# Attention blocks of 32 queries by 64 keys, four above each other, with v on both halves of the rows; rows of a stage's first slot requested ahead of weights

## The chip, the cores and the metric

The kernel runs on one core of one Trainium2 chip. Its metric is the device time of one execution, in microseconds. Five engines work side by side, each through its own list of instructions in order: TensorE (PE, whose weight loads are shown apart as PEld), VectorE (DVE), ScalarE (ACT), GpSimd (POOL) and SyncE (SP). SP mostly issues DMA transfers. Tiles live in SBUF (128 rows, or partitions); PE writes its results into eight banks of PSUM, from which DVE and ACT read them.

## What is computed

The reference is an attention block whose output feeds a mixture of experts:

- q, k, v are (batch 8, heads 8, 576 tokens, 64). Heads 0 to 3 attend to the 32 latest tokens. Heads 4 to 7 attend within 128 tokens to every fourth one, so with the tokens of equal remainder by 4 (a "strip" of 144) put together they too attend to the 32 latest of a strip.
- `attn = softmax(q @ k.T / 8 + mask)`, `attn @ v`, and the heads side by side give x of 4608 tokens by 512.
- `logits = x @ w_gate`, the largest of 8 picks an expert e, with the softmax's value as gate; `y = gate * (relu(x @ w1[e]) @ w2[e])`, w1 512 by 1024, w2 1024 by 512, all in f32.

## The kernel before, in words

A unit of attention is one pair of heads of one batch; there are 32, four to a batch: two with the plain mask (`ty` 0) and two with the strips (`ty` 1). `attention()` runs them as a software pipeline: in step i it normalizes unit i-1 (`norm`), computes the scores of unit i (`front`), the weighted sum of v of unit i-3 (`summed`) and the gate logits of unit i-4 (`logit_part`), transposes the weights of unit i-2 (`weights`, LAG is 2), turns q and k of unit i+1 (`turn`), writes rows for unit i-3 (`row_part`) and takes the exponentials of unit i (`exponentials`).

In `front` (L368) a unit's two heads lie on the two halves of the rows. Each has nine blocks of 64 queries by 96 keys (64 and the 32 ahead of them). PE is used as four arrays of 64 by 64: head r picks the half of the rows, the block's number the half of the columns (`place`). A head has one PSUM bank. For batches below EARLY (4) the mask is added on PE ahead of the scores (L356), and the exponentials read PSUM; for later batches DVE adds it (L390) and the exponentials read SBUF. ACT takes one exponential for each of nine columns of blocks (L405), with the sum as a by-product; POOL multiplies by the reciprocals (L420). `weights` makes nine transposes of 128 by 96 in three banks (L430), DVE copies each bank (L432). `summed` multiplies each block with its 96 rows of v (L445), which `load_v` brought in (L274, L277 and L290, on SP); ACT copies the two banks into xT (L459, L466). The PSUM banks go round among all tiles named `bank`, seven of them.

When a batch has ended, `route(b)` finds each token's expert and place and scatters the rows, with gate and number, into `bucket` in DRAM (L234); it is a generator, and the driver runs one piece of it after each piece of attention. `tables(s)` then lists the slots of stage s: a slot is 128 rows of one expert. `moe()` runs the slots: transposes of the rows (`across`, L1136), ph (64 matmul records, L1204), py (16 records of 512 columns, L1236), and a scatter to the output on POOL (L1253). Two slots out of all mix experts (L1166).

The order around the change is set by two things. First, the pacer at the end: each `yield` of `attention()` states a cost, and between two of them expert work is run at a rate (`clock`), counted in those costs; a stage's slots are spread over a given sum of costs. Second, `wanted`, an ordered list of rows ("x") and weights ("w1", "w2", in halves of 1 MB) with the number of finished layer halves that each waits for; `fetch` issues from its head only, on SP (rows of the last slots on ACT). SP is one queue in order: q, k, v, rows and weights all stand in it as they were issued.

At the start POOL issues five DMAs: the masks, the constants `cst`, and the gate's weights `wg`.

Of the kernel before, what the change touches and what calls it, by code (L numbers as in the profile page):

```python
# [69 lines left out]
LAG = 2  # L70
# [9 lines left out]
def _constants():  # L80


    def band(j, ty):

        qi, ki = 64 * j + np.arange(64)[:, None], max(0, 64 * j - WIN) + np.arange(96)[None]
        seen = (qi - ki >= 0) & (qi - ki < WIN)
        if ty:
            seen &= qi // STRIP == ki // STRIP
        return np.where(seen, 0.0, BIG)

    def mask(ty):

        pairs = [(0, 1), (2, 3), (4, 5), (6, 7), (8, 8)]
        return np.concatenate([np.concatenate([band(j, ty) for j in two]) for two in pairs], 1)
# [4 lines left out]


    parts = {"add0": mask(0)[:, 0:384], "add1": mask(1)}
    for name, ty, js in (
        ("even0", 0, (0, 2, 4, 6, 8, 8)), ("even1", 1, (0, 2, 4, 6, 8)), ("odd1", 1, (1, 3, 5, 7, 8))
    ):
        parts[name] = np.tile(np.concatenate([band(j, ty) for j in js], 1), (2, 1))
    parts["turn"] = np.tile(np.eye(64), (2, 1))

    exact, mask_at = [], {}
    for names in (("turn", "even0"), ("even1", "odd1"), ("add0", "add1")):
        n = 0  # L110
        for name in names:
            mask_at[name] = len(exact), n
            n += parts[name].shape[1]
        some = np.concatenate([parts[name] for name in names], 1).astype(np.float32)
        exact.append(np.ascontiguousarray(some.astype(ml_dtypes.bfloat16)))
    mask_at["odd0"] = mask_at["even0"][0], mask_at["even0"][1] + 96
# [45 lines left out]
def kernel(  # L162
# [91 lines left out]

    t = {}
# [12 lines left out]
    def first_key(j):  # L268
        return max(0, 64 * j - WIN)

    def load_v(b, ty):
        if ty == 0:
            x = pool.tile([96, 4, 9, DH], F32, tag="v0", name=f"v0_{b}", bufs=1)
            nc.sync.dma_start(x[:, :, 0, :], v[b, 0:4, 0:96, :].rearrange("h p d -> p h d"))  # L274
            for h in range(4):
                a = v[b, h, 64 - WIN : 160 - WIN, :]
                nc.sync.dma_start(  # L277
                    x[:, h, 1:9, :],
                    bass.AP(a.tensor, a.offset, [[DH, 96], [64 * DH, 8], [1, DH]]),
                )  # L280
        else:
            x = pool.tile([96, 2, 9, 2 * DH], F32, tag="v1", name=f"v1_{b}", bufs=1)
            for j in range(9):
                lo, end = first_key(j), first_key(j) + 96
                while lo < end:
                    hi = min(end, (lo // STRIP + 1) * STRIP)
                    h, m, at0 = lo // (2 * STRIP), lo // STRIP % 2, lo % STRIP
                    a = v[b, 4 + h : 5 + h, DIL * at0 + 2 * m : DIL * at0 + 2 * m + 1, :]
                    p0 = lo - first_key(j)
                    nc.sync.dma_start(  # L290
                        x[p0 : p0 + hi - lo, :, j, :],
                        bass.AP(
                            a.tensor,
                            a.offset,
                            [[DIL * DH, hi - lo], [2 * S * DH, 2], [1, 2 * DH]],
                        ),
                    )
                    lo = hi
# [39 lines left out]
    def place(r, j):  # L338

        return (4, r) if j == 8 else (5 * r + j // 2, j % 2)  # L340
# [3 lines left out]
    for j in range(0, 8, 2):  # L344
        ORDER += [(0, j), (1, j + 1), (0, j + 1), (1, j)]
    ORDER += [(0, 8), (1, 8)]

    def front(qT, kT, ty, early):
# [3 lines left out]
        for r in range(2) if early else ():  # L352
            rows = slice(DH * r, DH * r + DH)
            for c in range(2):
                n = 480 if c == r else 384
                nc.tensor.matmul(  # L356
                    sc[r][64 * c : 64 * c + 64, 0:n],
                    lhsT=mask("turn", rows, 64),
                    rhs=mask(("even", "odd")[c] + str(ty), rows, n),
# [4 lines left out]
        ends = [[max(j for j in range(9) if place(r, j)[1] == c) for c in range(2)] for r in range(2)]  # L364
        for r, j in ORDER:
            i, c = place(r, j)
            rows = slice(DH * r, DH * r + DH)
            nc.tensor.matmul(  # L368
                sc[r][64 * c : 64 * c + 64, 96 * (i % 5) : 96 * (i % 5) + 96],
                lhsT=qT[rows, 64 * j : 64 * j + 64],  # L370
                rhs=kT[rows, first_key(j) : first_key(j) + 96],
                start=not early,
                stop=not early or j == ends[r][c],
            )
        e = pool.tile([128, 9, 96], F32, tag="e", name="e", bufs=LAG + 1)
# [3 lines left out]
        for r in range(2):  # L379
            for i, n, p0, p1 in ((5 * r, 4, 0, 128), (4, 1, 64 * r, 64 * r + 64)):  # L380
                places.append((i, n, p0, p1, sc[r][p0:p1, 96 * (i % 5) : 96 * (i % 5 + n)]))
        for i, n, p0, p1, s in places:
            if early:
                nc.vector.tensor_reduce(  # L384
                    out=lo[p0:p1, i : i + n], in_=s.rearrange("p (i k) -> p i k", k=96),
                    axis=AX, op=OP.min,
                )
            else:
                at0 = 96 * (1 if (i, ty) == (4, 0) else i % 5)
# [3 lines left out]
                    in1=mask(f"add{ty}", slice(p0, p1), 96 * n, at0),  # L393
# [7 lines left out]
    def exponentials(e, lo, places):  # L401
        den = pool.tile([128, 9], F32, tag="den", name="den", bufs=3)
        for i0, n, p0, p1, s in places:
            for i in range(i0, i0 + n):
                nc.scalar.activation(  # L405
                    out=e[p0:p1, i],
                    in_=s[:, 96 * (i - i0) : 96 * (i - i0) + 96],
# [7 lines left out]
    def norm(e, den):  # L415
# [4 lines left out]
        nc.gpsimd.tensor_tensor(  # L420
# [938 lines left out]
```

## Time and profile before

| | us |
|---|---|
| median of 3 runs (842.04 to 842.5) | 842.38 |
| the profiled execution | 802.63 |
| its span, first to last instruction | 800.9 |
| PE busy in the span | 748.6 |
| DVE, ACT, POOL busy | 284.6, 225.5, 146.4 |
| granted TensorE clock, mean | 0.975 |
| attention alone, to unit 16's scores | 128.2 |
| attention and slots, from there to unit 31's scores | 300.2 |
| the rest | 372.5 |

The profile is of one execution, shorter than the timed runs; sums are made against its own time. A line of the groups names the source line, engine, operation, the tiles written and read, shapes, count, the busy time and the mean of one. On PE an f32 matmul stands as two records, each with a weight load; records overlap, so the distance from start to start tells more than the mean of one. In the table of windows each engine has its busy time and its instructions, then come the granted clock, DMA's busy share of 16 engines and GB/s.

### The profile page before, as it was taken

What the parts mean: (1) busy time and instruction counts of PE and PEld (TensorE: products, weight loads), DVE (VectorE), ACT (ScalarE), POOL (GpSimd) and SP (SyncE); (2) the same over time, 40 slices, a digit from 0 to 9 for tenths busy, and PEclk for the clock granted to TensorE, in tenths of its full rate; (3) what the DMA queues carried; (4) which work ended last, traced back from release to release, by engine and by line L of the source; (5) the groups of instructions that cost most, each with busy time, mean ns of one, the idle gap of its engine ahead of it and who ended that gap; (6) DMA issues with size and microseconds to landing.
All of it is one profiled execution on the core that took longest, in us unless ns stands there. A gap on an engine that the chain in (4) does not pass through costs nothing.

```text
span 800.9 us, 18005 instructions
## 1 busy us (share of the span) xinstructions
PE 748.6 (93%) x6838; PEld 559.4 (70%) x6838; DVE 284.6 (36%) x954; ACT 225.5 (28%) x853; POOL 146.4 (18%) x142
## 2 busy tenths in 40 slices
PE   4898898799997799999999999999999999999993
PEld 3787687488775577777777777768677374677681
DVE  1677878267334432354334411361101101101010
ACT  1896694253332132333333111000000011010000
POOL 1324433123211211113111300150000000000000
PEclk9999999899999799999999999999999999999997
DMA  9878689889999996799416937999992492993996
GB/s 200 178 157 196 156 233 370 190 242 281 281 305 279 359 265 193 253 311 313 147 58 199 279 122 228 309 355 383 328 319 82 150 330 97 320 307 122 332 309 219
DMA packets 164955, 195.39 MB, mean 244 GB/s; under 512 B 72720, under 2 KB 86688, under 8 KB 164866
## 3 DMA queue, kind: packets, MB, share of 16 engines
q1 hardware_dynamic: 153156, 169.00, 69.7%
q0 software_dynamic: 6928, 20.53, 7.2%
q10 hardware_dynamic: 4782, 4.67, 2.1%
q8 instruction: 57, 0.93, 0.5%
q14 instruction: 32, 0.26, 0.1%
HBM read 216.14 MB, written 21.54 MB: 297 GB/s over the span
## 4 chain that ended last, share of the span: by engine, by line
PE 79%; DMA 8%; ACT 5%; DVE 3%; issue 2%; another core or an unknown queue 1%; SPq 1%; POOL 0%; POOLq 0%; DVEq 0%; ACTq 0%
PE ph L1204 30%; PE py L1236 29%; PE xo L445 3%; ACT e L405 3%; PE scores L368 3%; PE weights L430 2%; DMA k<-in_k_dram 2%; DMA v<-in_v_dram 2%; PE xt L1136 2%; PE xrow L543 2%; DMA x<-bucket 2%; PE ph L1166 2%; PE py L1166 2%; PE turned L319 1%; DMA w<-in_moe_w_dram 1%
## 5 line engine op out<-in xcount | busy, mean ns | idle before, releaser
L1204 PEld LDWEIGHTS ph<-xt,w 128*128 128x128 f32 x2240 | 262.4, 193 | 19.5 <-issue 18.4
L1204 PE MATMUL ph<-xt,w 128*128 128x128 f32 x2240 | 271.7, 277 | 0.1
L1236 PE MATMUL py<-w,h 128*128 128x512 f32 x560 | 255.0, 598 | 0.0
L1236 PEld LDWEIGHTS py<-w,h 128*128 128x128 f32 x560 | 101.0, 191 | 101.4 <-issue 100.2
L1253 POOL DMA_INDIRECT out_dram<-y,to x35 | 34.6, 988 | 355.0 <-ACT y L1247 327.3
L1138 DVE COPY xt<-xt 128x512 f32<-128x512 f32 x38 | 26.1, 688 | 184.5 <-PE xt L1136 184.4
L1247 ACT ACTIVATE y<-py,x 128x512 f32<-128x512 f32 x35 | 24.0, 687 | 239.9 <-PE py L1236 177.6
L420 POOL TENSOR_TENSOR e<-e,rec 128x864 f32<-128x864 f32 x32 | 52.2, 1632 | 156.0 <-DVE rec L419 81.2
L432 DVE COPY eT<-weights 96x384 f32<-96x384 f32 x96 | 47.5, 545 | 39.8 <-PE weights L430 35.4
L405 ACT ACTIVATE e<-e,lo 128x96 f32<-128x96 f32 x144 | 51.8, 362 | 16.4 <-DVE lo L397 14.8
L234 POOL DMA_INDIRECT bucket<-rows,idx x48 | 44.5, 927 | 61.2 <-DVE idx L646 45.6
L405 ACT ACTIVATE e<-scores,lo 128x96 f32<-128x96 f32 (+1 forms) x160 | 52.5, 344 | 5.2 <-DVE lo L384 4.5
L445 PE MATMUL xo<-eT,v 96*64 96x64 f32 (+1 forms) x1216 | 45.2, 229 | 4.1 <-DMA v<-in_v_dram 4.1
L1224 DVE TENSOR_SCALAR h<-ph 128x512 f32<-128x512 f32 x35 | 24.1, 689 | 67.9 <-PE ph L1204 67.5
L445 PEld LDWEIGHTS xo<-eT,v 96*64 96x64 f32 x1216 | 40.5, 143 | 10.4 <-issue 6.6
L1215 ACT ACTIVATE h<-ph 128x512 f32<-128x512 f32 x35 | 20.8, 595 | 89.4 <-PE ph L1204 85.5
L312 ACT COPY kT<-turned 128x288 f32<-128x288 f32 x64 | 23.0, 414 | 80.2 <-PE turned L319 62.6
L430 PE MATMUL weights<-ident,e 128*96 128x128 f32 x288 | 39.2, 283 | 0.3 <-POOL e L420 0.3
L368 PE MATMUL scores<-kT,qT 64*64 64x96 f32 x1152 | 38.9, 267 | 0.1
L368 PEld LDWEIGHTS scores<-kT,qT 64*64 64x64 f32 x1152 | 33.5, 146 | 6.6 <-issue 5.0
L310 DVE TENSOR_SCALAR qT<-turned 128x288 f32<-128x288 f32 x64 | 26.5, 449 | 31.1 <-PE turned L319 16.5
L430 PEld LDWEIGHTS weights<-ident,e 128*96 128x96 f32 x288 | 32.6, 131 | 6.8 <-issue 5.7
(213 smaller groups left out, 594.2 us busy)
## 6 DMA issues: line engine op xcount, KB each, us to landing
w<-in_moe_w_dram SPq DMA_DIRECT2D x164, 1024.0 KB
x<-bucket SPq DMA_DIRECT2D x26, 257.0 KB
v<-in_v_dram SPq DMA_DIRECT2D x32, 192.0 KB
q<-in_q_dram SPq DMA_DIRECT2D x32, 144.0 KB
q<-in_q_dram SPq DMA_DIRECT2D x8, 576.0 KB
v<-in_v_dram SPq DMA_DIRECT2D x48, 96.0 KB
k<-in_k_dram SPq DMA_DIRECT2D x28, 144.0 KB
k<-in_k_dram SPq DMA_DIRECT2D x7, 576.0 KB
```

The source lines that it names most:

```text
L234: nc.gpsimd.indirect_dma_start(out=bucket, out_offset=bass.IndirectOffsetOnAxis(ap=idx, axis=0), in_=rows, in_offset=None, bounds_check=NR ...
L310: nc.vector.tensor_scalar(out, in_, -SCALE, None, op0=OP.mult)
L368: nc.tensor.matmul(sc[r][64 * c : 64 * c + 64, 96 * (i % 5) : 96 * (i % 5) + 96], lhsT=qT[rows, 64 * j : 64 * j + 64], rhs=kT[rows, first_ ...
L405: nc.scalar.activation(out=e[p0:p1, i], in_=s[:, 96 * (i - i0) : 96 * (i - i0) + 96], func=AF.Exp, bias=lo[p0:p1, i : i + 1], scale=-1.0, ...
L420: nc.gpsimd.tensor_tensor(out=e, in0=e, in1=rec.unsqueeze(2).broadcast_to([128, 9, 96]), op=OP.mult)
L430: nc.tensor.transpose(tp[0:96, 128 * i : 128 * i + 128], e[:, a + i], ident)
L432: nc.vector.tensor_copy(eT, tp[0:96, 0:384])
L445: nc.tensor.matmul(xo[DH * h : DH * h + DH, at0 : at0 + nq], lhsT=vt[:, 2 * hl + r, j, :] if ty == 0 else vt[:, hl, j, DH * r : DH * r + D ...
L1166: nc.tensor.matmul(out[mine], lhsT=lhsT[:, mine], rhs=ws[:, (j + (g >= KIND[mixed[j]])) % 2, c, cols], start=c == 0, stop=c == n - 1,)
L1204: nc.tensor.matmul(ph[:, fi], lhsT=w1[:, c, 128 * f : 128 * f + 128], rhs=xt[:, c], start=c == 0, stop=c == 3,)
L1236: nc.tensor.matmul(py, lhsT=h[:, f], rhs=w2[:, f], start=f == 0, stop=f == 7)
L1253: i = nc.gpsimd.indirect_dma_start(out=out, out_offset=bass.IndirectOffsetOnAxis(ap=to, axis=0), in_=y, in_offset=None, bounds_check=N - 1 ...
```

## The change

Blocks become 32 queries by 64 keys: 18 for a head, numbered as 9 to each half of its tokens (or strip). PE is used as eight arrays of 64 by 32 for the scores: four blocks stand above each other in a PSUM bank, 64 columns apiece. A strip's first block uses the keys of the next one, so that all blocks have 64. Two columns of blocks are transposed together, so that weights are five transposes of 128 by 128, and a block's 64 keys lie on the upper or the lower half of the rows; `load_v` puts the 64 rows of v that belong to a block on the same half. The weighted sum then is 36 matmuls of 32 columns on four arrays of 64 by 64, for 18 or 20 before, in two banks held together. The masks change shape with it.

Of the order: the constants, the third mask and wg are issued on POOL behind the first product. `route` has two more yields. The costs stated to the pacer are 2.2 for 3.0 and 0.6 for 1.1. In `wanted`, the rows of slots 1 to J0+1 (J0 is the last stage's first slot) are put four entries earlier, first slots of stages too; slot 1's weights wait for the first half of slot 0's first layer; and `fetch` passes over rows whose stage isn't known yet.

```diff
 def load_v(b, ty):
+    x = pool.tile([128, 4, 2, 5, DH], F32, tag=f"v{ty}", name=f"v{ty}_{b}", bufs=1)
+    ...
+    for m in range(ty, 9):
+        j = m + 9 * (m == 0)
+        half, s0, n = at_v(j, ty)
+        lo, end = first_key(j, ty), first_key(j, ty) + 64
+        while lo < end:
+            if ty == 0:
+                a, hi = v[b, 0:1, lo : lo + 1, :], end
+                step = [[DH, 64], [S * DH, 4] if s0 else [9 * 32 * DH, 8], [1, DH]]
+            else:
+                hi = min(end, (lo // STRIP + 1) * STRIP)
+                row = DIL * (lo % STRIP) + 2 * (lo // STRIP)
+                a = v[b, 4:5, row : row + 1, :]
+                step = [[DIL * DH, hi - lo], [S * DH, 4], [1, 2 * DH]]
+            p0 = 64 * half + lo - first_key(j, ty)
+            ...
 def place(r, j):
-    return (4, r) if j == 8 else (5 * r + j // 2, j % 2)
+    s, m = divmod(j, 9)
+    return (8, 2 * r + s) if m == 8 else (4 * r + 2 * s + m // 4, m % 4)
 ORDER = []
-for j in range(0, 8, 2):
-    ORDER += [(0, j), (1, j + 1), (0, j + 1), (1, j)]
-ORDER += [(0, 8), (1, 8)]
+for j in (0, 4, 9, 13):
+    for c in range(4):
+        ORDER += [(0, j + c), (1, j + (c ^ 1))]
+ORDER += [(0, 8), (1, 17), (0, 17), (1, 8)]
 def front(qT, kT, ty, early):
     ...
             nc.tensor.matmul(
-                sc[r][64 * c : 64 * c + 64, 96 * (i % 5) : 96 * (i % 5) + 96],
-                lhsT=qT[rows, 64 * j : 64 * j + 64],
-                rhs=kT[rows, first_key(j) : first_key(j) + 96],
+                sc[r][32 * c : 32 * c + 32, at0 : at0 + 64],
+                lhsT=qT[rows, 32 * j : 32 * j + 32],
+                rhs=kT[rows, first_key(j, ty) : first_key(j, ty) + 64],
 def weights(e):
-    for a in range(0, 9, 3):
-        tp = bank("weights")
-        for i in range(3):
-            nc.tensor.transpose(tp[0:96, 128 * i : 128 * i + 128], e[:, a + i], ident)
-        eT = pool.tile([96, 384], F32, tag="eT", name="eT", bufs=4)
-        nc.vector.tensor_copy(eT, tp[0:96, 0:384])
+    eT = pool.tile([128, 5, 128], F32, tag="eT", name="eT", bufs=2)
+    tp = bank("weights", 4, 128)
+    for i in range(4):
+        nc.tensor.transpose(tp[:, i], e[:, 2 * i : 2 * i + 2].rearrange("p i k -> p (i k)"), ident)
+    nc.vector.tensor_copy(eT[:, 0:4], tp)
+    tp = bank("weights")[:, 0:128]
+    nc.tensor.transpose(tp, e[:, 7:9].rearrange("p i k -> p (i k)"), ident)
+    nc.vector.tensor_copy(eT[64:128, 4], tp[64:128])
 def summed(eT, b, xT, ty, hl):
     ...
+        TURN = ((0, 0, 0), (1, 1, 1), (1, 1, 0), (0, 0, 1), (0, 1, 0), (1, 0, 1), (1, 0, 0), (0, 1, 1))
+        ...
+            nc.tensor.matmul(
+                xo[half][DH * h : DH * h + DH, at0 : at0 + 32],
+                lhsT=vt[rows, 2 * hl + r, s2, n] if ty == 0 else vt[rows, hl, s2, n, DH * r : DH * r + DH],
+                rhs=eT[rows, i // 2, 32 * c : 32 * c + 32],
 def attention():
-        nc.gpsimd.dma_start(cst, ...)
-        load_masks(2)
-        nc.gpsimd.dma_start(wg[:, :, 0:E], ...)
     ...
+                product = norm(evs[i - 1], dens.pop(i - 1))
+                if i == 1:
+                    with tc.issue_after(product.ins):
+                        nc.gpsimd.dma_start(wg[:, :, 0:E], ...)
+                        nc.gpsimd.dma_start(cst, ...)
+                        load_masks(2)
     ...
-            yield 3.0, ended
+            yield 2.2, ended
     ...
-                yield 1.1, None
+                yield 0.6, None
 def route(b):
         nc.vector.tensor_copy(lgs, logits.pop(b))
+        yield
     ...
         yield
+        yield
         ps = bank("rank")
 wanted:
+        if j == 1:
+            w = [(j, what, 0, max(1, n)) for _, what, _, n in w]
         if j - 1 in mixed:
             wanted.insert(len(wanted) - 2, x)
-        elif j < J0 and j not in firsts:
-            wanted.insert(len(wanted) - 4, (j, "x", 1, 2 * j - 6))
+        elif 0 < j < J0 + 2:
+            wanted.insert(len(wanted) - 4, (j, "x", 1, max(0, 2 * j - 6)))
 def fetch():
-        while wanted and wanted[0][0] in where and done[wanted[0][2]] >= wanted[0][3]:
-            j, what, _, _ = wanted.pop(0)
+        while wanted:
+            at0 = 0
+            while at0 < len(wanted) - 1 and wanted[at0][1] == "x" and wanted[at0][0] not in where:
+                at0 += 1
+            j, what, layer, n = wanted[at0]
+            if j not in where or done[layer] < n:
+                return
+            wanted.pop(at0)
```

## The prediction

> **What bounds the kernel now.** I read the page's shares and slices first, then the timeline of TensorE (PE) in one unit of attention, then the chain that ended last for its longest single steps, then the table of windows. A "unit" is one pair of heads of one batch; there are 32, numbered from 0.
>
> ```profile
> span 800.9 us, 18005 instructions
> PE 748.6 (93%) x6838; PEld 559.4 (70%) x6838; DVE 284.6 (36%) x954; ACT 225.5 (28%) x853; POOL 146.4 (18%) x142
> ...
> DMA  9878689889999996799416937999992492993996
> ```
>
> PE is busy 93% of the span; DMA is at 0.9 or more in most slices up to about 380 us, so it stands close behind PE exactly where attention runs. The second reading is what PE does in one unit (start, length):
>
> ```profile
> 37.34 1.03 PE L368 MATMUL scores<-kT,qT 64*64 64x96 f32 x36
> 38.30 1.27 PE L445 MATMUL xo<-eT,v 96*64 96x64 f32 x36
> 39.50 1.19 PE L430 MATMUL weights<-ident,e 128*96 128x128 f32 x9
> 40.52 0.66 PE L319 MATMUL turned<-ident,q 96*128 96x96 f32 x6
> ```
>
> Start to start: scores 0.96 us, xo 1.20, weights 1.02, together 3.18 us of a unit's 5.5 or so on PE. A matmul in f32 stands as two records. Two single steps in the chain (start, length) are DMA waits that PE sat through:
>
> ```profile
> 128.58 16.98 DMA v<-in_v_dram
> ...
> 251.00 14.82 DMA x<-bucket
> ```
>
> The timeline of PE shows idle stretches of 4.14 us before xo at 145.70 and 10.41 us before xt at 265.87. Windows between the starts of units 4, 8, 12, 16 and 31 (span, PE, PEld, DVE, ACT, POOL, clock, DMA, GB/s):
>
> ```profile
> 37.30:65.50 28.20, 24.77 (x462) 20.85 (x462) 21.55 (x66) 21.83 (x102) 8.00 (x5) 0.99 0.77 166
> 65.50:95.70 30.20, 26.48 (x464) 22.55 (x460) 22.54 (x73) 21.46 (x101) 12.41 (x11) 0.95 0.76 174
> 95.70:128.20 32.50, 29.28 (x480) 25.33 (x474) 26.86 (x99) 21.84 (x102) 13.70 (x13) 0.92 0.90 264
> 128.20:428.40 300.20, 285.21 (x2795) 221.50 (x2794) 128.93 (x395) 99.95 (x375) 59.47 (x55) 0.97 0.83 249
> ```
>
> So there are three stages: attention alone (to 128), attention mixed with expert slots (to 428), slots alone (372.5 us more, PE full).
>
> **What the Trainium skill says.** "TensorEngine Tiling (Array Packing)", Available Configurations: a 64x64 array has 4 tiles, a 64x32 one has 8, and tiles run in parallel. "TensorE: Matmul & The Clock Gate", The mechanism, puts packed matmuls about 4 ns apart. The same page ("Wait — 56ns, not 53.3ns?") gives about 25 ns as the least start to start. The trace lies between: 36 scores in 0.96 us, about 0.17 of it the drain before xo, are 21 to 22 ns each over four tiles; xo's 36 over two tiles take 29. Both are what a tile's own repeat gives (512 columns take 429 ns in the py row of the chain, 6.87 us for 16, so 96 columns 80 ns over four tiles, 64 columns 54 over two). No stretch of this trace needs more than one record per 20 ns for long, so whether eight tiles can be fed is not shown. "DMA: Bandwidth & Descriptors", Why small descriptors are slow, says small pieces pay a fixed part; here a 256-byte packet takes 22 ns and a 2 KB one 100.
>
> **Part 1, PE work of a unit.** Scores: 36 matmuls, 72 records, of 64 columns on eight tiles. Floor: 9 rounds of 57 ns = 0.51 + 0.17 drain = 0.68 us. At the rate already seen (20 ns a record, some 20 waiting ready) 1.38. xo: 72 records of 32 columns on four tiles: floor 18 rounds of 30 ns + 0.15 = 0.69, at 20 ns 1.6. Weights: 5 transposes for 9, at 109 ns = 0.59 (saved 0.43, sure). Sum 1.96 to 3.6 against 3.18: from -1.2 to +0.4 us a unit. I take 11 to 12 ns a record, between the floor and the seen rate, since the bursts in the trace (four records within 20 ns) show quick dispatch: 2.5 us, **-0.7 a unit**. Of 16 mixed units 11 us; the masks (eight small bf16 matmuls for four) stay within 0.05 us.
>
> **Part 2, the other engines.** Exponentials: 64 columns for 96; the copies of xT (320 columns 426 ns, 256 columns 370) give 0.9 ns a column, so 9 x 28 ns = 0.25 us saved on ACT a unit, and one more copy (about 0.2) in every second unit: ACT stays near 5.4 us a unit. DVE: eT copies 3 x 545 become about 690 + 250, saved 0.7. POOL: the product 1632 ns becomes about 1090. None of them was full (ACT 77%, DVE 76% in the first window), so I count these at nothing but as slack; if PE's cover went, ACT would set 5.4 to 5.6 a unit.
>
> **Part 3, v.** Each batch loads v as 64-row pieces: 4352 packets of 256 bytes for 3456 and 2048 of 512 for 1728, 22 and 30 ns over 16 engines = 1.2 + 0.6 = **1.8 us of DMA a batch**. SP issues 19 DMAs for 18, at about 0.5 us, so no change there. A batch of the first stage needs 28.2 x 0.77 = 21.7 to 30.2 x 0.76 = 23 us of DMA, then 23.5 to 25.
>
> **Part 4, start.** wg, cst and the third mask go behind the first product on POOL. That takes some 0.35 MB out of the first 15 us (DMA is 0.97 busy in the first 20, so about 1 to 2 us). But the two row writes that need cst stand on POOL ahead of unit 1's product: product at 23, three issues (1.9 us), cst 7.8 us to land: about 32 instead of 28.5. Behind it PE waits in order: unit 1's transposes (L430 of before), and with them the scores of unit 4. I let gain and loss cancel: unit 4 at 37; with the cover of the lighter start gone it is 3 us worse, with cst landing in 4 us it is 2 better.
>
> **Part 5, route.** Two more yields put other work between lgs and its transposes and before rank, where the timeline shows PE idle 0.88, 1.10 and 1.19 us: 2 us a batch in the first stage.
>
> **First stage.** A batch: 28.2 to 32.5 less 2.8 (PE) less 2 is 24 to 27.5, DMA allows no less than 25 or so; 26, 26, 27: unit 16 at **116** instead of 128.
>
> **Part 6, fetch order and pace.** Weights of slot 1 now wait for slot 0's first half, so 4 MB and not 8 stand ahead of v of batch 3 on SP; they move past that v, q and k of batches 4 and 5 and v of batch 4, 40 or so issues, and are needed only at slot 1, which by the built order comes at about unit 20, four units on; rows of slots up to J0+1 are asked for four loads earlier, so the 14.8 us wait for x goes. What follows on SP is the weights, half a us later, with a whole slot in hand. The stages around the two waits took 22 us more than their slots and units should (units 17 to 18 took 22.7 us with 8.6 of expert work, 22 to 24 took 56.5 with 30.6; 6 us is a unit). By the built order, unit 31 now finds 155.9 us of expert matmuls done where it found 188.4, since the units' costs to the pacer are lower: 32.5 us (2.3 slots) are moved behind attention, at 14.45 a slot 33.5.
>
> **Mixed stage.** PE: 300.2 - 186.6 of expert work = 113.6; less 22 of stalls, less 11, is 81; plus 155.9 = 237. DMA: 300.2 x 0.83 = 249 + 7 for v, less what is prefetched beyond unit 31, about 13: 243, and it was never above 0.99 for long. I take **246**: DMA becomes as near as PE. Unit 31 starts at 362.
>
> **Last stage.** 372.5 + 33.5 - 2 (three units' tails) = 404. Sum 116 + 246 + 404 = 766 of span, **35 us less**; with the 1.7 around it 768 against the profiled 802.63. The runs' median is 842.38, 1.05 times as much, which nothing in the trace explains; scaled 806, shifted 808. I say 806.
>
> **Rivals.** (B) Eight tiles are fed at the floor and DMA hides: -1.2 a unit, first stage 113, mixed 228, 745 in all, 782 scaled. For it: the bursts. Against: DMA at 0.9.
> (C) DMA becomes the bound of the mixed stage: 256 at 0.97 = 264, unit 16 at 118: 118 + 264 + 404 = 786, 826 scaled; a rate of 20 ns a record ends there too. For it: slots with new weights need 4 MB (about 12.9 us of DMA) per 14.45.
> (D) Slower: PE takes small records no faster than in one tile. Gain and loss meet near +1.2 us a unit, that is (3.18 + 1.2 - 0.59 - 0.32) / 144 = 24 ns a record. Served one after another (57 and 30 ns) the unit would take 3.6 us more, and 32 units over 70 us net: 910. Against: four tiles already run at 21.
> (E) The waits only move: x and v come on time and the next w is late, 15 us back: 822; in C's range.
>
> **How the numbers follow.** Likeliest 0.5 (own range 794 to 818), B 0.15, C with E 0.25, D 0.1. A difference under 0.2% can't be told from none here. Faster 0.88, within 0.2% 0.02, slower 0.1. The range 782 to 834 leaves out D and the fast end of B.
>
> **What would show it.** Right: 72 scores records in some 0.9 us and 72 xo in about 1.0; no idle stretch before xt near 250; unit 16 near 116 and unit 31 near 362; DMA near 0.95 between. Wrong: records at 20 ns or more; PE waiting for w in the mixed stage; POOL's second product later than 33 us pushing all of the first stage.

## The result

The changed kernel is slower: 893.8 us (888.52 to 894.71, four runs) beside 842.21 us, ratio 1.060, 95% interval 1.056 to 1.064. The forecast was 806. In a later comparison it gave 893.71 beside 841.57 (1.062, 1.058 to 1.066). In another, two of its four runs fell in a slower state of the chip (902.79 and 904.02 us) and are left out; the other two gave 885.36 and 891.68 beside 840.87.

Of the page of the profile of the changed kernel (called the profile after), the span, the shares of PE, the clock in 40 slices, and the queue that brings instructions (packets, MB, share of 16 engines):

```profile
span 892.5 us, 22371 instructions
PE 789.8 (88%) x9014; PEld 584.9 (66%) x9014; DVE 253.8 (28%) x922; ACT 216.5 (24%) x869; POOL 130.7 (15%) x142
PEclk9677878699899799998999899979999999999998
q8 instruction: 74, 1.21, 0.6%
```

PE was busy 93% of the span and is busy 88%, so the engine that bounds the kernel is used less. Its clock is under nine tenths in eight of the first thirteen slices, where before all but one stood at 9. In the second line, 9014 matmul records with 9014 weight loads are 18028 PE instructions; before they were 13676, and 57 packets of instructions came for these 74. The groups of instructions (busy time, mean ns | idle time before, and what ended it):

```profile
L463 PE MATMUL xo<-eT,v 64*64 64x32 f32 x2304 | 64.5, 233 | 32.9 <-issue 32.8
L380 PE MATMUL scores<-kT,qT 64*32 64x64 f32 x2304 | 42.9, 242 | 14.0 <-issue 13.5
...
L573 PE MATMUL logits<-xT,wg 128*32 128x192 f32 x192 | 19.0, 364 | 6.3 <-ACT xT L477 5.8 <-ACT xT L482 0.4
```

"issue" means that PE waited for nothing the profile shows: no semaphore, no transfer. 46 us of it stand before scores and xo, where the first profile of before had none. The wait for rows x that took 10.41 us of PE before xt is gone. The third row is a new wait, for the copies of xT.

The kernel before was profiled again (first experiment), on a chip where it takes what its timed runs take. That profile, and not the first one, is what the changed kernel has to be held against. Its two groups:

```profile
L445 PE MATMUL xo<-eT,v 96*64 96x64 f32 (+1 forms) x1216 | 50.0, 233 | 10.7 <-issue 10.5
L368 PE MATMUL scores<-kT,qT 64*64 64x96 f32 x1152 | 40.6, 265 | 5.5 <-issue 5.3 <-ACT kT L312 0.2
```

And the tables of windows, to the starts of units 4, 16 and 31 and to the end (span, PE, PEld, DVE, ACT, POOL, clock, DMA, GB/s), of the second profile of before and of after:

```profile
0.00:38.80 38.80, 23.44 (x299) 19.21 (x300) 14.96 (x50) 19.10 (x93) 8.66 (x14) 0.96 0.87 185
38.80:144.70 105.90, 85.81 (x1398) 72.96 (x1398) 71.11 (x239) 65.85 (x305) 34.80 (x29) 0.90 0.75 190
144.70:453.40 308.70, 296.10 (x2794) 228.27 (x2793) 128.65 (x393) 100.02 (x375) 58.93 (x54) 0.95 0.80 237
453.40:841.00 387.60, 364.53 (x2354) 253.44 (x2353) 70.05 (x275) 41.01 (x81) 43.84 (x45) 0.98 0.73 245
```

```profile
0.00:40.90 40.90, 22.61 (x494) 18.74 (x502) 14.16 (x48) 18.73 (x94) 8.34 (x15) 0.87 1.04 182
40.90:155.90 115.00, 90.72 (x2220) 76.34 (x2204) 59.18 (x212) 62.81 (x309) 25.49 (x26) 0.78 0.66 170
155.90:466.20 310.30, 275.74 (x3588) 209.61 (x3587) 109.48 (x385) 91.15 (x378) 51.58 (x54) 0.91 0.76 228
466.20:892.50 426.30, 400.71 (x2726) 280.20 (x2725) 71.02 (x279) 43.78 (x88) 45.27 (x47) 0.97 0.69 237
```

DMA is less busy than before in every stage but the start, so it is not the bound. PE's idle time, span less busy, went from 71.1 to 102.7 us; its busy time grew by 19.9, at a lower clock. These two make up the 51.5 us between the two spans.

**Two ways in which PE stands still.** The first shows in the timeline of PE in the profile after, here in two units of the first stage (start, length, operation, count, idle before):

```profile
42.22 1.28 PE L463 MATMUL xo<-eT,v 64*64 64x32 f32 x38
46.52 1.38 PE L463 MATMUL xo<-eT,v 64*64 64x32 f32 x34 [3.02 <-issue]
...
59.56 1.11 PE L463 MATMUL xo<-eT,v 64*64 64x32 f32 x58
63.11 0.55 PE L463 MATMUL xo<-eT,v 64*64 64x32 f32 x14 [2.44 <-issue]
```

PE stops in the middle of a group that needs nothing more. The trace's single records of PE and of the instruction queue explain it. PE's instructions come in packets of 16 KB, 256 instructions each. The packet that ends the first stop began at 43.75 and took 1.2 us; the other began at 60.44 and took 1.35. At those moments PE had executed 1217 and 1985 instructions, both 193 more than a multiple of 256, and the same holds for the stops at 100, 190, 258, 332 and 355 us: each time PE had used up everything that had been delivered, and went on 1.3 to 1.6 us after the next packet had landed. These seven stops are 18 us of idle time. A unit's scores and xo are 288 instructions within 2.3 us. In the kernel before they are 144 to 152, and no packet found PE without at least 80 in hand. I call this the fetch running dry, and such a stop a dry stop.

The second way is seen beside the runs of six scatters of rows into the bucket. The timeline of PE and POOL in the profile after:

```profile
215.88 0.71 PE L380 MATMUL scores<-kT,qT 64*32 64x64 f32 x46
216.19 0.94 POOL L234 DMA_INDIRECT bucket<-rows,idx  x1 [4.45 <-DVE idx L664]
217.43 0.92 POOL L234 DMA_INDIRECT bucket<-rows,idx  x1 [0.30 <-issue]
217.51 0.32 PE L380 MATMUL scores<-kT,qT 64*32 64x64 f32 x5 [0.44 <-issue]
218.25 0.33 PE L380 MATMUL scores<-kT,qT 64*32 64x64 f32 x4 [0.42 <-issue]
219.00 0.34 PE L380 MATMUL scores<-kT,qT 64*32 64x64 f32 x5 [0.42 <-issue]
```

From the first scatter on, PE gets about five matmuls with their loads, ten instructions, every 0.73 us: 14 a us. The 72 scores that take 0.97 us elsewhere take 6.4 here. The second profile of before has the same stalls, the first has none. The scores of one unit beside the scatters of the same batch, in the second and in the first:

```profile
287.61 0.72 PE L368 MATMUL scores<-kT,qT 64*64 64x96 f32 x22
288.63 0.32 PE L368 MATMUL scores<-kT,qT 64*64 64x96 f32 x2 [0.30 <-issue]
290.07 0.32 PE L368 MATMUL scores<-kT,qT 64*64 64x96 f32 x3 [1.12 <-issue]
...
276.01 1.04 PE L368 MATMUL scores<-kT,qT 64*64 64x96 f32 x36
```

Counted from each batch's first scatter to 3 us after its last, PE's idle time in all is 31 us in the second profile of before and 41 after. So of the 31.6 us of idle time that the change adds, 18 are dry stops and 10 stand beside scatters.

**The clock follows.** The table of windows of PE after the second stop (span, PE, clock, DMA, GB/s):

```profile
59.00:62.00 3.00, 1.67 (x108) 1.00 1.23 223
62.00:65.00 3.00, 1.89 (x27) 0.92 0.20 34
65.00:68.00 3.00, 3.00 (x22) 0.51 0.58 167
68.00:71.00 3.00, 3.00 (x160) 1.00 0.39 105
```

After 2.44 us of idle the clock is half for some 3 us, in which PE stands as fully busy. In the clock's own record each stretch at half clock within the work lasts 3.41 us or a multiple of it, and five of the seven dry stops run into one, or are followed by one within 1.6 us (the stop at 43.5 us fell into one that had begun before it). The Trainium skill, "TensorE: Matmul & The Clock Gate", Part 1: The HAM clock gate, says that PE falls to half clock after an idle window of about 3.4 us and comes back after as long a busy one. The trace agrees on the half clock and the time to come back; less idle than 3.4 us sufficed here. Since the record has only full and half, the time at half clock is about 2 x (1 - mean clock) x span: 74 us in the second profile of before, 143 after.

### The profile page after: what moved, and what is told of

Its sections match the earlier page's. It is cut to its first block, busy times and chain, and to the rows that moved or that the text cites. A ratio compares the mean times of both kernels' runs of the same rounds, so it can differ in the third digit from the quotient of the medians.

```text
span 892.5 us, 22371 instructions
## 1 busy us (share of the span) xinstructions
PE 789.8 (88%) x9014; PEld 584.9 (66%) x9014; DVE 253.8 (28%) x922; ACT 216.5 (24%) x869; POOL 130.7 (15%) x142
## 4 chain that ended last, share of the span: by engine, by line
PE 78%; issue 8%; DVE 4%; ACT 3%; DMA 2%; SPq 2%; another core or an unknown queue 1%; POOLq 0%; POOL 0%; ACTq 0%; DVEq 0%
PE ph L1231 28%; PE py L1263 25%; PE xo L463 6%; PE scores L380 3%; PE xrow L559 2%; PE turned L330 2%; PE xt L1163 2%; ACT e L416 2%; PE weights L440 2%; PE ph L1193 2%; PE py L1193 2%; PE turned L338 2%; PE logits L573 2%; SPq L306 1%
## 5 line engine op out<-in xcount | busy, mean ns | idle before, releaser
L1280 POOL DMA_INDIRECT out_dram<-y,to x35 | 34.5, 986 | 422.0 <-ACT y L1274 410.6
L463 PE MATMUL xo<-eT,v 64*64 64x32 f32 x2304 | 64.5, 233 | 32.9 <-issue 32.8
L463 PEld LDWEIGHTS xo<-eT,v 64*64 64x64 f32 x2304 | 54.8, 149 | 43.2 <-issue 38.4
L431 POOL TENSOR_TENSOR e<-e,rec 128x576 f32<-128x576 f32 x32 | 36.8, 1149 | 226.8 <-DVE rec L430 171.7
L380 PE MATMUL scores<-kT,qT 64*32 64x64 f32 x2304 | 42.9, 242 | 14.0 <-issue 13.5
L416 ACT ACTIVATE e<-scores,lo 128x64 f32<-128x64 f32 (+1 forms) x160 | 48.0, 312 | 20.6 <-DVE lo L396 18.9
L416 ACT ACTIVATE e<-e,lo 128x64 f32<-128x64 f32 x144 | 47.9, 337 | 3.9 <-DVE lo L408 3.9
L380 PEld LDWEIGHTS scores<-kT,qT 64*32 64x32 f32 x2304 | 33.9, 114 | 21.7 <-issue 18.9
L443 DVE COPY eT<-weights 128x512 f32<-128x512 f32 x32 | 22.0, 688 | 44.3 <-PE weights L440 36.1
L564 DVE COPY rows<-xrow 96x384 f32<-96x384 f32 x32 | 17.6, 550 | 53.8 <-PE xrow L559 53.5
L416 ACT ACTIVATION_READ_ACCUMULATOR e<-scores,lo 128x1 f32 (+1 forms) x160 | 32.6, 204 | 0.0
```

What stands on the lines that cost most here:

```text
L380: nc.tensor.matmul(sc[r][32 * c : 32 * c + 32, at0 : at0 + 64], lhsT=qT[rows, 32 * j : 32 * j + 32], rhs=kT[rows, first_key(j, ty) : first ...
L416: nc.scalar.activation(out=e[p0:p1, i], in_=s[:, 64 * (i - i0) : 64 * (i - i0) + 64], func=AF.Exp, bias=lo[p0:p1, i : i + 1], scale=-1.0, ...
L431: return nc.gpsimd.tensor_tensor(out=e, in0=e, in1=rec.unsqueeze(2).broadcast_to([128, 9, 64]), op=OP.mult)
L463: nc.tensor.matmul(xo[half][DH * h : DH * h + DH, at0 : at0 + 32], lhsT=vt[rows, 2 * hl + r, s2, n] if ty == 0 else vt[rows, hl, s2, n, DH ...
L1280: i = nc.gpsimd.indirect_dma_start(out=out, out_offset=bass.IndirectOffsetOnAxis(ap=to, axis=0), in_=y, in_offset=None, bounds_check=N - 1 ...
```

## The experiments

All 18 runs are below. The kernel before took 841 to 842 us on the chips of all comparisons but one, and 802.91 on the chip of that one (the kernels with halves, with half the passes, thinned, and with scatters of their own); ratios are to before on the same chip. Where the time lies in the profiles (stages as in the windows; PE idle is span less busy; us):

| kernel | start | first | mixed | last | span | PE idle | at half clock |
|---|---|---|---|---|---|---|---|
| before, first profile | 37.3 | 90.9 | 300.2 | 372.5 | 800.9 | 52 | 40 |
| before, second profile | 38.8 | 105.9 | 308.7 | 387.6 | 841.0 | 71 | 74 |
| order alone | 33.8 | 102.5 | 303.3 | 402.6 | 842.2 | 67 | 84 |
| blocks alone | 41.3 | 125.2 | 316.1 | 392.4 | 875.0 | 92 | 133 |
| changed, costs as before | 40.3 | 115.7 | 314.8 | 402.1 | 872.9 | 93 | 106 |
| changed | 40.9 | 115.0 | 310.3 | 426.3 | 892.5 | 103 | 143 |
| before, wide | 37.1 | 106.8 | 295.9 | 375.5 | 815.3 | 57 | 44 |
| blocks alone, wide | 43.0 | 124.9 | 310.2 | 373.8 | 851.9 | 86 | 97 |
| changed, wide | 41.3 | 117.3 | 293.3 | 410.8 | 862.7 | 89 | 107 |

**The kernel before again.** No edit.

> The kernel before, unchanged, for a second profile: its first profiled execution took 802.63 us, its timed runs 842. If 802.63 is what the kernel does when TensorE is never short of instructions and 842 is what it does otherwise, this profile takes about 842, with a clock of about 0.93 and idle stretches of PE that stand as issue and sum to some 30 us. If the first profile was only disturbed in its clock (or the timed runs are slower for a reason outside the trace), the idle stretches of PE are as in the first, 52 us, and the span 801 or so. Ratio 1.00 in both.

Measured: 841.23 us (10 runs), ratio 0.999; the profiled execution took 842.8. The first reading holds, with smaller numbers: some 23 us of idle as issue, 16 of them before scores and xo and 6 before ph, beside the scatters; the mean clock is 0.956. The 803 and the 842 us belong to different chips: on the chip of the fifth to eighth kernel here, 20 runs of before lie between 798.82 and 808.26, and on the others none is under 837. The chip of the first profile is not on record; its time and the missing stalls are those of the 803 us chip. The idle time before xt, where the first profile waited 10.41 us for x, is 1.2 us here.

**Blocks alone.** The kernel before with the changed `front`, `weights`, `summed`, `load_v` and masks, and nothing else.

```diff
-                for part in range(2):
-                    summed(eTs[u], b2, xTs[u], ty2, hl2, part)
+                summed(eTs.pop(u), b2, xTs[u], ty2, hl2)
```

> Only the blocks of 32 queries with their masks, v and products; fetch order, route, start and the pacer's costs as before. Theory 1 (TensorE runs out of instructions: a unit issues 288 small records in some 2.3 us where it issued about 150, and PE stands still until the next packet of 256 lands): the whole loss is here, 890 to 915, PE idle before xo and scores as issue, 40 us or more. Theory 2 (the order of transfers and of expert work costs it): within 1% of before, 835 to 850. Theory 3 (v in more packets holds up DMA): 855 to 870, the longest idle stretches before xo end with v.

Measured: 877.9 us, 1.042 (1.038 to 1.046). That is between the ranges of theories 1 and 3. The sign is theory 1's: PE is idle as issue before scores and xo for 34 us and never waits there for v; six stops are dry, for 13 us.

> Blocks alone, a repeat beside the changed kernel. On the 842 chip 878. On the 803 chip: 823 to 840 if PE's fetch runs dry as often as there (6 times), 800 to 810 if it doesn't.

The repeat gave 874.68 beside 841.57, 1.040 (1.035 to 1.045). So 33 to 36 of the 52 us are the blocks.

**Order alone.** The kernel before with the late `cst` and `wg`, the two yields and the new `wanted` and `fetch`; costs 3.0 and 1.1.

```diff
-        elif j < J0 and j not in firsts:
-            wanted.insert(len(wanted) - 4, (j, "x", 1, 2 * j - 6))
+        elif 0 < j < J0 + 2:
+            wanted.insert(len(wanted) - 4, (j, "x", 1, max(0, 2 * j - 6)))
```

> Only the order: wg, cst and the third mask behind the first product, the two yields in route, rows asked for ahead of weights; blocks of 64 queries with 96 keys and the pacer's costs as before. Theory 1: the waits for v and x that it takes away were worth about 22 us in the first profile, so 815 to 835. Theory 2: as slow as the changed kernel, 880 or more. If the waits only move (rival E of the prediction): 842 within 0.5%.

> Order alone, a repeat. On the 842 chip 845. On the 803 chip the kernel before waits some 11 to 15 us for rows x near 260, which this should take away: 785 to 797; if the wait only moves, 800 to 806.

> Order alone once more. Where before takes 803 us, it waits 11 to 15 us for rows x near 260: 0.98 to 0.99 of before; if the wait only moves, 0.997 to 1.004. On an 842 chip 1.005 as before.

Measured in three comparisons: 1.0045 (1.002 to 1.007), 1.006 (1.004 to 1.008), 1.005 (1.003 to 1.006). Theory 1's 815 to 835 is wrong: there was no wait for x to be taken away on these chips. The table shows what the order does do: the start is 5 us earlier, the first stage 3 and the mixed one 5 shorter, and the last stage 15 longer, one slot of expert work that is now left for it. How it would do where the wait for x exists stays open: none of the three fell on such a chip.

**The costs to the pacer.** The changed kernel with

```diff
-            yield 2.2, ended
+            yield 3.0, ended
...
-                yield 0.6, None
+                yield 1.1, None
```

> The changed kernel with a unit's costs to the pacer put back to 3.0 and 1.1, so that as much expert work stands between two units as before. Theory 1: the small records come as densely within a unit as in the changed kernel, so idle as issue changes little; fewer units behind each other without expert work: 880 to 895. Theory 2 (expert work moved behind attention leaves attention bare): 850 to 865.

Measured: 879.36 us, 1.0445 (1.041 to 1.048): 14 us under the changed kernel, between the two theories. With the lower costs the last stage is 24 us longer (402.1 to 426.3), and the mixed stage, from which that work is taken, only 4.5 shorter: without wide matmuls between its units, PE runs dry there at 190, 258, 332 and 355 us, with the higher costs only at 335. Blocks 36, order 4 and costs 14 make 54, within 3 us of the whole.

**As many instructions, the old tiles.** The kernel before with each scores matmul cut in two of 48 keys and each xo matmul in two of half the queries.

```diff
-            nc.tensor.matmul(
-                xo[DH * h : DH * h + DH, at0 : at0 + nq],
+            for x in range(0, nq, nq // 2):
+                nc.tensor.matmul(
+                    xo[DH * h : DH * h + DH, at0 + x : at0 + x + nq // 2],
```

> The kernel before with each scores matmul cut into two of 48 keys and each xo matmul into two of half its queries: as many PE instructions as the changed kernel has, and none of its tiles, v or masks. Theory 1 (the number of PE instructions in a short time costs the time): scores and xo take 0.2 to 0.3 us more a unit where PE is fed, some 8 us in all, and PE is idle before them as issue for 30 us or more (16 in the kernel before): 870 to 890. Rival (the small tiles, their weights or v do it): only the 8 us, 845 to 855, idle as before.

Measured on the 803 us chip: 833.5, ratio 1.041 (1.032 to 1.049). The ratio is what theory 1 gave, and its reason is wrong: PE is hardly idle, it is busy. The group:

```profile
L453 PE MATMUL xo<-eT,v 96*64 96x32 f32 (+1 forms) x2432 | 82.1, 224 | 3.7 <-issue 3.7
```

xo took 43.7 us in a run of the kernel before's tiles on the same chip. In the records, the two tiles take their next matmul every 58 ns with 32 columns, as they do with 64: a tile repeats a load and a matmul no faster. A unit's 72 pairs over two tiles then take 2.31 us, where 36 take 1.27. The fetch ran dry twice, for 2.8 us; that 300 instructions over 3.6 us are less dense than the changed kernel's is the likely reason, not a tested one.

**Half the passes.** Blocks alone, with q, k and the weights written in bfloat16 and v rounded by POOL. It leaves out the precision of f32, so only its times are of use.

```diff
-        dst = pool.tile([128, S], F32, tag=name + "T", ...)
+        dst = pool.tile([128, S], BF16, tag=name + "T", ...)
...
+                    nc.gpsimd.tensor_copy(*[... for y in (vb, x)])
```

> Only the blocks (as in the run with blocks alone, 878), with scores and xo in bfloat16: q, k and the weights are written so by the copies that are there, v is rounded by one POOL copy more a batch and type; the output is rounded. One pass each, so 72 PE instructions for 144. Theory 1: the idle stretches before scores and xo (34 us as issue with the blocks alone) fall below 12, and some 0.5 us a pass and unit is saved besides: 800 to 825. Rival (number of instructions is not it): the passes save up to 1.1 us a unit, 35 in all, and the idle stays: 843 to 855.

Measured on the same chip: 805.75, 1.003 (1.001 to 1.006). The edit brought a wait of its own, so the time decides nothing; the groups do:

```profile
L463 PE MATMUL xo<-eT,vb 64*64 64x32 bf16 x1152 | 23.2, 190 | 58.2 <-POOL vb L515 56.9 <-issue 1.2
```

57 us of PE's idle time end with POOL's copy of v. Idle as issue is 1.2 us before xo and none before scores, and the two passes take 0.45 and 0.50 us. With half the instructions at the same tiles PE is fed; but so it nearly is in the next run on this chip, with all of them, so this one does not tell the number of instructions from their place.

**Thinned.** Blocks alone, the transposes of weights, q and k moved between a unit's scores and xo.

```diff
             evs[i], lo, places = front(qT["q"], qT["k"], units[i][1], units[i][0] < EARLY)
+            yield 1.5, None
+            ... weights(i - LAG), turn(i + 1)
             ... summed(u), logit_part(u - 1)
-            yield 3.0, ended
-            ... weights(i - LAG), turn(i + 1)
+            yield 1.5, ended
             ... row_part(u)
```

> Only the blocks, with the transposes of weights, q and k (some 70 large PE instructions, 2.3 us) and a stop for expert work put between scores and xo of a unit. No PE work added or removed. Theory 1 in the form that the instructions come too densely (288 in 2.3 us, more than a packet of 256): fewer stalls, idle as issue before scores and xo below 25, 855 to 868. Rival (their number counts, not where they stand, or it is the scatters alone): 873 to 882.

Measured on the same chip: 822.97, 1.027 (1.020 to 1.033), so the blocks in this order lose there too; in their own order they were not run on this chip. Idle as issue is 3 us before xo and none before scores; the fetch ran dry twice, for 5 us. In place of it, xrow waits 12 us for the copies of xT, since it now follows xo at once. This run also gives the blocks' PE work where PE is fed: scores 37.6, xo 50.9, weights 22.4 us; the next one gives the old blocks' on the same chip, 38.5, 43.7 and 38.3. That is 9.6 us less in 32 units, 0.3 us each.

**Scatters of their own.** The kernel before with 24 more indirect scatters and 24 plain stores on POOL.

```diff
+            for n in range(24) if j == NSLOT - 15 else ():
+                i = nc.gpsimd.indirect_dma_start(out=spare[0], ...)
+            for n in range(24) if j == NSLOT - 9 else ():
+                nc.gpsimd.dma_start(spare[1][128 * n : 128 * n + TT], blank[0:TT])
```

> The kernel before with 24 indirect scatters of 96 rows more, to memory of their own, in the last stage, and six slots later 24 plain stores of the same rows; both on POOL. If the indirect scatters starve TensorE of instructions: PE idle as issue in the slots beside the first 24, 5 us or more, none beside the second 24, 848 to 860. If the stalls beside scatters only coincide with them: no idle at either place, 842 within 0.5%. If any load on the DMA queues does it: both places.

Measured: 814.67, 1.017 (1.010 to 1.024). It tells nothing on its question: nothing held the scatters back, so POOL issued them between 10 and 49 us, ahead of its products, for which PE's transposes then waited 5.8 us; and the chip was the one on which no scatter stalls PE.

**The changed kernel beside a thinned one.** `a0_after` and `a3_after` are the changed kernel unedited. The other is the changed kernel with the old costs, and a unit's PE work in the order scores, transposes of q and k, xo, transposes of weights, xrow.

```diff
             evs[i], lo, places = front(qT["q"], qT["k"], units[i][1], units[i][0] < EARLY)
+            yield 1.5, None
+            ... turn(i + 1)
             ... summed(u), logit_part(u - 1)
-            yield 2.2, ended
-            ... weights(i - LAG), turn(i + 1)
+            yield 1.5, ended
+            ... weights(i - LAG)
             ... row_part(u)
```

> The changed kernel again, beside the next three on one chip. Two chips have been seen: one on which the kernel before takes 842 us and PE is short of instructions beside the scatters into the bucket, one on which it takes 803 and is not. On the first: 893 as before. On the second: without the stalls beside scatters (some 35 us) but with PE's fetch running dry at some 8 places (20 us): 825 to 845 against 803, that is 3 to 5% slower. If the loss was only the scatters' stalls: 795 to 808.

> The changed kernel with a unit's costs as before, and PE's work of a unit put in another order: scores, transposes of q and k, xo, transposes of weights, xrow, so that large instructions stand between the small ones and xrow doesn't follow xo at once. If the places where fetch runs dry are the loss: 2 to 3% under the changed kernel, at the kernel before or under it: 0.975 to 1.0 of before. If the number of small records is the loss wherever they stand: 1.03 to 1.045 of before.

> The changed kernel once more, for a chip on which the kernel before takes 803 us. There, from the run with thinned blocks (1.027 of before) and 20 us of fetch stalls in place of its 3: 1.03 to 1.05 of before. If the fetch stalls hide behind other work there: 1.00 to 1.02. On an 842 chip: 1.06 as before.

Measured: the changed kernel 893.71 (1.062, 1.058 to 1.066) and, in the other comparison, 885.36 and 891.68 us; neither fell on the 803 us chip. Thinned 877.66, 1.0455 (1.040 to 1.051), level with the 879.36 of the same kernel not thinned. But this order did not take the dry stops away: PE used up the delivered instructions at six places, for 12 us in all, against four places and 10 us not thinned. Idle as issue is still 28 us before xo, much of it beside the scatters, where xo now stands. So this order is no cure on these chips, and what a kernel without dry stops would gain stays untested.

**Scatters under wide matmuls.** Each batch's scatters wait until a slot's first layer is done, and the slot's second layer is put beside them on PE.

```diff
+        while not phase["py"]:
+            step()
+        with tc.issue_after(phase["relu"].ins):
+            yield
+        while phase["py"]:
+            step()
...
-        for i in range(NT):
-            to_bucket(idx[:, i : i + 1], row[:, i], b)
+        with wide_only():
+            for i in range(NT):
+                to_bucket(idx[:, i : i + 1], row[:, i], b)
```

> The kernel before, but each batch's scatters into the bucket, from the fourth batch on, are held until a slot's first layer is done, and the slot's second layer (matmuls of 512 columns, 2.3 PE instructions a us) is put beside them on PE. If PE is starved beside scatters because it is given about 14 instructions a us there: the stalls of the mixed and last stage (2.4 to 6.6 us a run, 18 in all, and as much again in halved clock) go: 810 to 830 where before takes 842. If scatters stop PE whatever it does: 838 to 848. Where before takes 803 us: 0.995 to 1.01 in both.

> The same with the order of the changed kernel (starts, route, rows asked ahead), blocks of 64 queries as before. Where before takes 842 us: what the run with scatters under wide matmuls alone gives, plus 3 us. Where it takes 803 us: 0.98 to 0.99 of before if the wait for x goes, 1.00 if not.

Measured: 816.13 us beside 840.87, ratio 0.969 (0.965 to 0.973); with the new order too 812.78, 0.969 (0.964 to 0.974). Both beat both kernels. The timeline of POOL and of PE at the scatters of the seventh batch:

```profile
458.65 0.94 POOL L234 DMA_INDIRECT bucket<-rows,idx  x1 [5.97 <-DVE idx L670]
...
464.80 0.92 POOL L234 DMA_INDIRECT bucket<-rows,idx  x1 [0.30 <-issue]
460.04 7.03 PE L1264 MATMUL py<-w,h 128*128 128x512 f32 x16
```

Six scatters pass while PE does 16 matmuls of 512 columns in 7.03 us, without a gap: 32 instructions, under 5 a us, are less than the 14 a us that it gets (the 2.3 of the expectation leave out the weight loads). The stalls stay where there is no expert work to put there (some 4 us of idle at each of the first three batches). So the stalls follow from how many instructions PE needs at that time. Why the supply is slow beside scatters on some chips and not on another, no run here shows.

**The same for the changed kernel.**

> The changed kernel with the scatters into the bucket under a slot's second layer, as in the run before that took the kernel before from 841 to 816. If its loss is all in stalls beside scatters: 812 to 825, level with that run. If the fetch running dry (20 us idle) and the clock after it cost most: 850 to 870.

> Only the blocks, with the scatters so placed. Of the 36 us that the blocks cost, the stalls beside scatters are hardly longer than before (38 us against 35), so most should stay: 838 to 856. If the scatters' stalls are the loss: 812 to 825.

Measured: changed 858.87 (1.018, 1.015 to 1.020), blocks alone 850.85 (1.009, 1.007 to 1.012). Placing the scatters so takes some 25 us from before and from the blocks alone, and some 35 from the changed kernel; with 15 us of idle left beside scatters in all three, the blocks still cost 35 us (851 against 816) and the changed kernel 43. That rules these stalls out as the main cause of the difference. What is left for the blocks alone is 18 us in the first stage, 14 in the mixed one and 6 at the start, with twice as much time at half clock (97 against 44 us). The blocks alone have 28 us more idle time here than before, and nine dry stops make 19 of it; before has none. In the changed kernel there are twelve, for 29 of its 31.5 us more. In the mixed stage of the blocks alone 11 of some 12 us more idle time are dry stops. The profile puts the longest, 4.9 us, down to weights w; it too comes where all delivered instructions are used up and ends 1.4 us after a packet landed.

## Why the prediction was wrong

**The step that failed** is Part 1. It took 11 to 12 ns a record, and wrote that "whether eight tiles can be fed is not shown"; but its worst case was 20 ns a record, which is a rate. What the trace shows is a supply: PE takes 288 instructions of a unit at a high rate until the delivered ones are used up, and then stands for 1.6 to 4 us while a packet comes, and mostly its clock halves. That is in no term of the sum. Over 32 units Part 1's worst case, +0.4 a unit, is 13 us; the blocks cost 33 to 36. That the dry stops are the largest part of it is read from the traces (18 of 31.6 us more idle time, 19 of 28 with the scatters under wide matmuls); no run removed them alone.

**Its size where PE is fed** was off too: -0.3 us a unit for -0.7, and 16 ns a record in the mean for 11 to 12. Weights came out a little better than written (0.70 us a unit for 1.20, -0.5 for -0.43). Scores take 0.97 us for 72 records, near the forecast's 0.9: eight tiles do run at once, their records 6.7 ns apart within a round, so the 25 ns that the prediction cites from the Trainium skill's "TensorE: Matmul & The Clock Gate" are no floor across tiles. xo takes 1.37 us where "about 1.0" was written, over a floor of "18 rounds of 30 ns": a round takes 58 ns with 32 columns as with 64.

**Part 2** counted the copies of xT at nothing, as slack on ACT. Before, the first copy ran while PE filled the second bank; now both banks are finished together, and logits wait for both copies: 6.3 us in all.

**Part 3** was right: 256-byte packets are now 69376 for 62208, at 20.7 and 21.5 ns; 512-byte ones 16384 for 13824, at 34.5 and 30.5. That is 1.9 us of DMA a batch for 1.8. It didn't matter, with DMA at 0.66 in the first stage and 0.76 in the mixed one.

**Parts 4 and 5.** Part 4 let gain and loss cancel; with the order alone unit 4 comes 5 us earlier, at 33.8 for 38.8. Part 5 had the right sign there: 3.4 us less in the first stage where 6 were written. With the blocks unit 4 is at 40.9, not 37: PE waits 12 us in all for q at the turns, one wait of 5.69 us near 30 us.

**First and mixed stage**: unit 16 at 156 for 116, unit 31 at 466 for 362. Here the dry stops, the stalls beside scatters and the half clock come in. From the second profile of before to after, idle time adds 31.6 us and busy time 19.9. The work where PE is fed is 9.6 less, so some 30 us of busy time would be the price of 69 us more at half clock; this split is an estimate.

**Part 6** removed 22 us of stalls that only the first profile had. It moved expert work behind attention as written: the last stage is 38.7 us longer than in the second profile, forecast +31.5. But the mixed stage gave none of it back: 310.3 us for 308.7, where 246 for 300.2 was written. With the costs put back the kernel is 14 us faster, so this part failed too.

**The time base.** The prediction scaled by 1.05, "which nothing in the trace explains". That was the place to stop: the first profile is one without the stalls beside scatters and with a wait for x, and the chips on which both kernels were timed against each other have it the other way round. The 22 us of removed stalls came from it.

**The rivals.** D had the sign and not the mechanism: small records are not served one after another; where PE is fed, a unit's 144 records take 2.34 us, 16 ns each, and D had 24. C and E named DMA and the next w; DMA is less busy than before.

## What to carry to other kernels

When work is cut into smaller matmuls, count PE's instructions per us beside their columns: 288 in 2.3 us ran dry of packets of 256, and most stops were paid twice, as idle time and then at half clock. Put work that needs few instructions, such as 512-column matmuls, beside anything that slows the supply; here that alone was worth 3%. And if the profiled time differs by 5% from the timed runs, profile again before building on its waits.

## What the runs showed of the hardware that was not expected

- PE's instructions come in 16 KB packets of 256, which take about 1.1 us; after a stop PE goes on 1.3 to 1.6 us after the landing.
- Beside indirect scatters issued by POOL (0.92 us each) PE gets about 14 instructions a us on chips where the kernel before takes 842 us; on one where it takes 803, no such stall is seen.
- A tile repeats a weight load with its matmul every 58 ns, with 32 columns as with 64; over eight tiles records start 6.7 ns apart within a round. Of a unit's 72 scores the first 32 start within 0.27 us, the rest 12 ns apart in the mean, and all take 0.97 us.
- The same program takes 4.6% less time on one chip than on others, with the same packets and nearly the same time a packet (2 KB: 98 to 100 ns on the one, 98 to 101 on the others).
